# Windowed attention joined to a Mish MLP on one core: the first two pairs' scores, exponentials and squares stand beside the first layer, and the second layer has four attention visits in place of five

## The chip, the cores and the metric

The kernel runs on one core of a Trainium2 chip. The metric is the device time of one execution in microseconds (us). Before the change it is 1049.76 us, the median of three runs. The engines are named as in the profile: PE (TensorE's matmuls) and PEld (its weight loads), DVE (VectorE), ACT (ScalarE), POOL (GpSimd) and SP (SyncE, whose queue issues all the DMAs here).

## The reference

```python
B, H, S, D = 8, 8, 576, 64
scores = scale * np.matmul(q, k.transpose(0, 1, 3, 2))
bias = slopes[:, None, None] * (-np.abs(rel))[None, :, :]
mask = (rel >= 0) & (rel < 128)
scores = np.where(mask, scores + bias[None], -1000000000.0)
attn = np.exp(scores - np.max(scores, axis=-1, keepdims=True))
attn = attn / (np.sum(attn, axis=-1, keepdims=True) + 1e-09)
x = (attn @ v).transpose(0, 2, 1, 3).reshape(B * S, H * D)      # 4608 x 512
h = x @ w_in                                                    # 512 x 2048
sp = np.where(h > 20.0, h, np.log1p(np.exp(np.minimum(h, 20.0))))
out = (h * np.tanh(sp)) @ w_out                                 # 2048 x 512
```

Attention looks back over 127 positions at most, so each block of 128 queries meets 192 keys at a time. The MLP's weights come as 64-bit numbers.

## The kernel before

**Two halves of the work.** The attention of one batch gives 576 rows of x. 512 of them go through the MLP as one unit `c`; the last 64 queries of every batch are kept in DRAM (`xs`) and make a ninth unit, `c` = 8. A unit has a **first layer**, eight chunks `j` of 24 matmuls 128x512 into `h` (`first(c, j)`), each followed by a Mish on ACT (`mish`, g<-h); and a **second layer**, 32 steps of 6 matmuls into `po0` and `po1` (`second`), 16 for each half of the rows. What the second layer multiplies is prepared by `parts`: a rounded copy on ACT and a remainder on POOL (both gg<-g), three buffers. A finished `po0` or `po1` is copied to `ob` and stored; each has one bank.

**Attention of the next batch stands inside the unit.** `attention(b)` makes the steps of the four pairs of heads `p` of batch `b` = `c` + 1, for `c` = 1 to 6. A pair goes through these steps, in two groups `g` of blocks:

- `scores`: 36 matmuls 64x64 with `qk`. Pair 0 writes the banks `o`, `w`, `po0`, `po1`; the others write `s`, whose two buffers the first layer's `h` uses too.
- `bias`: twelve DVE instructions, pz<-s,nb, into the tile `pz` (tag `pz`, two buffers, one for each group).
- `exp`: nine ACT instructions in place, each with a sum. `divide` and `scale`: the sums plus 1e-9 (ACT), their reciprocal (DVE), the product (POOL).
- `turn` and `move_out`: DVE transposes squares of 32 in place, and three DMAs write `pz` to DRAM (`d`). `move_in`: six DMAs read `d` back as the transposed weights, into `pta` and `ptb`, which have one buffer each.
- `rest_values` and `values`: 60 small matmuls of `pta` and `ptb` with `v` into `o` and `w`. `keep` copies the last 64 queries to `xo` and stores them in `xs`; `split_x` makes the MLP's input x from `o` and `w` (ACT and DVE).

**Where they stand.** PE and SP work through the program in its written order; on DVE, ACT and POOL the framework's scheduler orders the instructions when the kernel is built. Pair 0's scores and biases are written ahead of the first layer's last chunk. Everything else is sorted into the 32 steps of the second layer by a number:

```python
VISITS = (2.0, 10.0, 16.5, 23.0, 29.9)
def when(x):
    k = min(max(int(x // 1), 0), 3)
    return VISITS[k] + (VISITS[k + 1] - VISITS[k]) * (x - k)
```

So pair 1's scores come at step 2.0, the values of pair 0 and the scores of pair 2 at 10.0, the values of pair 1 and the scores of pair 3 at 16.5, and the values of pairs 2 and 3 at 23.0 and 29.9. A pair's `move_in` and the loads of a later pair's `qk` are written shortly behind such a visit, and `keep` ahead of them. `v` of pairs 0 and 1 is loaded at the start of the second layer, into the tiles from which the first layer read x.

**The start.** Batches 0 and 1 and the MLP of unit 0 follow an order written out by hand (`FIRST_STEPS`), on all engines; the weights are converted to two rounded parts there (cE, cW, cU, cL: ACT and DVE, ACT, POOL, with tiles `ti`, `wi`, `si`; `to`, `wo`, `so` for the second layer's). In it, `lC0` to `lC3` copy the last queries of batch 0's pairs to `xo` (three buffers), and `lbS0` to `lbS3` are batch 1's scores of the last queries: matmuls of a block of `qk`, 128 columns called the corner, that stands behind q and k in each `qk` tile of 640 KB. The `xs` stores stand in SP's queue behind the loads of all weights but one.

Of the kernel before, what the change touches and what calls it, by code (L numbers as in the profile page):

```python
# [8 lines left out]
F32 = mybir.dt.float32  # L9
# [7 lines left out]
P = 128  # L17
# [63 lines left out]
def attention_mish_mlp(  # L81
# [23 lines left out]
    B, NP, _, QKZ = qk_.shape  # L105
    NT, DM = out.shape
    S = NT // B
# [7 lines left out]
    LEFT = S - CH  # L115
# [49 lines left out]
    def load(dst, src):  # L165
        sp.dma_start(out=dst, in_=src)
# [90 lines left out]
    qkv = {}  # L257
# [10 lines left out]
    def parts_of(t):  # L268

        qk = t[:, : 2 * S].rearrange("p (a s) -> p a s", a=2)  # L270
        return lambda h, n0, n: qk[h, 0, n0 : n0 + n], lambda h, n0, n: qk[h, 1, n0 : n0 + n], t[:, 2 * S : QKZ]

    def tables_of(t, l):
        return t.bitcast(BF16).rearrange("p (i n) -> p i n", i=2), l.bitcast(BF16)

    def load_first(p):

        t = tiles[p]
        if p > 1:
            n = QKZ + TAB + LAST  # L280
            load(t[:, :n], qk23[p - 2])
            qkv[(0, p)] = (*parts_of(t), *tables_of(t[:, QKZ : QKZ + TAB], t[:, QKZ + TAB : n]))
            return


        pieces = []
        n = 0
        for k in (CH, TAB, 6 * P, P, LAST):
            pieces.append(t[:, n : n + k])
            n += k  # L290
        a, tab, b, z, l = pieces
        load(a, qka[p])
        load(tab, tabs[p])
        if p == 0:
            load(b, qkb0)
        else:
            load(last_of(tiles[0]), last0)
            load(t[:, CH + TAB : n], qkb1)
        q = lambda h, n0, n: a[h, n0 : n0 + n] if n0 < 256 else b[h, n0 - 256 : n0 - 256 + n]
        k = lambda h, n0, n: a[h, 256 + n0 : 256 + n0 + n] if n0 + n <= 256 else b[h, 192 + n0 : 192 + n0 + n]  # L300
        qkv[(0, p)] = (q, k, z, *tables_of(tab, l))
# [3 lines left out]
        return t[:, n : n + P + LAST]  # L305

    def load_pair(b, p):
        t = at.tile([P, QKZ], F32, tag="qk", name=f"qk{b}_{p}")
        load(t, qk_[b, p])
        qkv[(b, p)] = parts_of(t)  # L310

    def load_v(b, p):

        pl, tag = (at, "pta") if (b, p) == (0, NP - 1) else (xp, f"x{p}")
        t = pl.tile([P, 2, 4, P], F32, tag=tag, name=f"v{b}_{p}", bufs=1)
        load(t, v[b, p])
        qkv[("v", b, p)] = ((t[:, 0], t[:, 1]), t[:64, 1, 3])

    def score_banks(name):
        return ps.tile([P, 2, 512], F32, tag="s", name=f"s{name}", bufs=2)  # L320
# [159 lines left out]
    def last_unit(p):  # L480
# [3 lines left out]
        name = f"{b}_{p}l"  # L484

        def scores():
            _, keys, z = qkv[(b, p)]

            t = qkv[("s", b, p)] = score_banks(f"{b}_{p}_0")
            st["s"] = t[:, :, :96]  # L490
            for a in range(2):
                for r in HEAD:
                    pe.matmul(
                        st["s"][r, a, :], lhsT=z[:, r], rhs=keys(slice(0, P), 384 + 96 * a, 96),
                        start=True, stop=True, skip_group_check=True,
                    )
# [54 lines left out]

        def keep():
            o = st["o"]
            xo = at.tile([P, LEFT], F32, tag="xo", name=f"xo{name}", bufs=3)
            dve.tensor_copy(xo, o)
            sp.dma_start(out=xs[p, :, b * LEFT : (b + 1) * LEFT], in_=xo)

# [10 lines left out]
    def pair_steps(b, p):  # L568
# [9 lines left out]
            return 256 * a if g == 0 else (384, 192)[a]  # L578

        def scores(g):  # L580
            if p == 0:

                tags = ("po0", "po1") if g else "ow"
                s_ = [ps.tile([P, 512], F32, tag=x, name=f"{x}s{name}") for x in tags]
            else:
                t = score_banks(f"{name}_{g}")
                s_ = [t[:, i, :] for i in range(2)]
            st[g]["s"] = s_
            q, k, _ = qkv[(b, p)]
            for a, j in enumerate(GROUPS[g]):  # L590
                for u in range(2):
                    q0 = j * P + 64 * u
                    k0, n = (q0 - WINDOW, SPAN) if j else (0, P)
                    for i in range(2):
                        pe.matmul(
                            s_[i][HALF[u], group_col(g, a) : group_col(g, a) + n],
                            lhsT=q(HEAD[i], q0, 64), rhs=k(HEAD[i], k0, n),
                            start=True, stop=True, skip_group_check=True,
                        )
            if g:  # L600
                for i in range(2):
# [136 lines left out]
                )  # L738

        def keep():  # L740
            xo = at.tile([P, LEFT], F32, tag="xo", name=f"xo{name}", bufs=3)
            dve.tensor_copy(xo, qkv[("o", b, p)][1][:, 2 * P : 2 * P + LEFT])
            sp.dma_start(out=xs[p, :, b * LEFT : (b + 1) * LEFT], in_=xo)

# [11 lines left out]
        exps = [[(lambda g=g, a=a, i=i: block_exp(g, a, i)) for a in ((1, 0) if g else (0, 1)) for i in range(2)] for g in range(2)]  # L756
        biases[1].insert(2, last_bias)
        exps[1].insert(2, last_exp)
        begin = [lambda: scores(0), lambda: scores(1)]
        if p == 0:  # L760
            begin += biases[0] + biases[1]
            both = [(0.8 + 0.05 * g, f) for g in range(2) for f in exps[g]]
        else:
            both = [(0, begin[0]), (0.001, begin[1])]
            both += [(0.01 + 0.05 * g, f) for g in range(2) for x in zip(biases[g], exps[g]) for f in x]
        d = 0.7 if p == 0 else 0
        both += [
            (d + 0.12, lambda: divide(0)), (d + 0.125, lambda: scale(0)),
            (d + 0.2, lambda: divide(1)), (d + 0.21, lambda: scale(1)),
            (d + 0.3, lambda: turn(0)), (d + 0.31, lambda: move_out(0)),  # L770
            (d + 0.45, lambda: turn(1)), (d + 0.46, lambda: move_out(1)),
            (d + 0.6 if p == 0 else 1.01, lambda: move_in(0)), (d + 0.7 if p == 0 else 1.02, lambda: move_in(1)),
            (2.002, rest_values), (2.003, values), (2.01, keep), (2.02, split_x),
        ]
        return begin, both

    def first_attention():

# [102 lines left out]
        def last_queries(p):  # L881
# [56 lines left out]
                        )  # L938

            def keep():  # L940
                xo = at.tile([P, LEFT], F32, tag="xo", name=f"xo{name}", bufs=3)
                dve.tensor_copy(xo, st["o"])
                sp.dma_start(out=xs[p, :, :LEFT], in_=xo)

# [13 lines left out]

    def attention(b):

        VISITS = (2.0, 10.0, 16.5, 23.0, 29.9)

        def when(x):
            k = min(max(int(x // 1), 0), 3)
            return VISITS[k] + (VISITS[k + 1] - VISITS[k]) * (x - k)

        steps = []
        for p in range(NP):
            begin, rest = pair_steps(b, p)
            if p == 0:  # L970
                first_scores = begin
            steps += [(when(p - 1 + d), f) for d, f in rest]
            nxt = (b, p + 2) if p + 2 < NP else (b + 1, p + 2 - NP)
            if nxt[0] < B:
                steps.append((when(p - 0.97), lambda nxt=nxt: load_pair(*nxt)))

        steps += [(d, lambda p=p: load_v(b, p)) for p, d in enumerate((-0.5, -0.4, 4.0, 17.5))]
        return first_scores, sorted(steps, key=lambda s: s[0])

    def last_x():  # L980
        c = B
# [161 lines left out]
    for name in FIRST_STEPS.split():  # L1143
        steps[name]()
        if name in loads:
            loads[name]()
        if name == f"Q{NJ - 1}":
            load_w(*last_w)
            add_conversions(range(len(conv) - 2, len(conv)))
            for p in range(2):  # L1150
                load_v(1, p)
    dve.fixed = act.fixed = pool.fixed = False

    for c in range(1, B + 1):
        for j in range(NJ):
            if j == NJ - 1:
                parts(c, 0, 0)
                parts(c, 0, 1)
                if c + 1 < B:
                    first_scores, beside = attention(c + 1)  # L1160
                    for f in first_scores:
                        f()
            if c > 1 or j > 2:
                first(c, j)
            if c > 1 or j > 1:
                mish(c, j)

        n = 4 * NJ
        steps = []
# [3 lines left out]
            if m >= 2:  # L1173
                steps.append((2 * m - 4.1, lambda m=m: parts(c, *divmod(m, NJ))))
        if c + 1 < B:
            steps += beside
        elif c + 1 == B:
            steps.append((4.5, last_x))
        for _, work in sorted(steps, key=lambda s: s[0]):
# [89 lines left out]
```

## Time and profile before

| | us |
|---|---|
| Three runs | 1045.5, 1049.76, 1049.86 |
| Profiled execution: its own time | 1039.15 |
| Its span, first to last instruction | 1037.4 |
| PE busy in the span | 952.7 |
| First layer of unit 3, with pair 0's scores | 45.26 |
| Second layer of unit 3, with attention | 72.64 |
| Second layer of unit 7, without attention | 43.52 |

The profiled execution is 1.75 us longer than its span, and 10.6 us shorter than the runs' median. PE is busy for 92% of the span, and what it waits for is read layer by layer: the first layers and the second layers are different stages, and so is the start.

### The profile page before, as it was taken

To read this page: it belongs to the slowest core of one execution; us is meant where nothing else is said; L and a number is where in the kernel's file an instruction comes from. 1 tells how busy PE (TensorE), PEld (TensorE's weight loads), DVE (VectorE), ACT (ScalarE), POOL (GpSimd) and SP (SyncE) were. 2 spreads that over 40 slices of the span, in tenths; PEclk is the share of its full clock that TensorE was granted. 3 is DMA by queue.
4 is the path that set the end of the run, shared out by engine and by line. 5 is a ranking of instruction groups with operands and counts; after the bars stand their busy time and mean duration, and the time that the engine had idled before them with its cause. 6 is when DMAs were issued, how large, how long until landed. Compare 5 with 4: busy or idle time off the path is not lost.

```text
span 1037.4 us, 17207 instructions
## 1 busy us (share of the span) xinstructions
PE 952.7 (92%) x6650; PEld 778.0 (75%) x6650; DVE 286.9 (28%) x1119; ACT 403.3 (39%) x1051; POOL 330.1 (32%) x300
## 2 busy tenths in 40 slices
PE   9859999979899799979899799979899799999998
PEld 7648788867788677867788577867788688888886
DVE  6568861135101530134101530134101530100000
ACT  7668752155123532155123432155123433221221
POOL 5438751044211541044211540044211541042032
PEclk9969999998999899989999899998999899999999
DMA  9941320045501661054501661055501651000001
GB/s 350 398 166 49 110 91 23 26 156 154 148 1 67 178 203 38 28 168 136 152 1 67 177 203 37 26 162 144 154 0 67 198 146 43 21 21 21 1 1 40
DMA packets 89217, 108.20 MB, mean 104 GB/s; under 512 B 22704, under 2 KB 69296, under 8 KB 89136
## 3 DMA queue, kind: packets, MB, share of 16 engines
q1 hardware_dynamic: 89136, 107.11, 32.6%
q8 instruction: 52, 0.85, 0.3%
q14 instruction: 29, 0.24, 0.1%
HBM read 76.94 MB, written 30.15 MB: 103 GB/s over the span
## 4 chain that ended last, share of the span: by engine, by line
PE 52%; issue 16%; DMA 14%; SPq 6%; DVE 5%; ACT 3%; POOL 3%; DVEq 0%; POOLq 0%; ACTq 0%
PE h L69 25%; PE po L69 21%; DMA d<-pz 7%; SPq L69 6%; DVE pz L69 4%; DMA pta<-d 3%; DMA wi<-in_moe_w_in_dram 2%; PE o L69 2%; PE w L69 2%; POOL pz L69 2%; PE s L69 2%; DMA nb<-in_relb_dram 1%; POOL gg L69 1%; ACT pz L69 1%; ACT g L69 1%
## 5 line engine op out<-in xcount | busy, mean ns | idle before, releaser
L69 PE MATMUL po<-so,gg 128*128 128x512 f32 x1728 | 411.5, 396 | 6.8 <-POOL gg L69 6.0
L69 PE MATMUL h<-x,si 128*128 128x512 f32 x1728 | 398.7, 392 | 17.3 <-ACT g L69 17.3
L69 PEld LDWEIGHTS h<-x,si 128*128 128x128 f32 x1728 | 325.1, 189 | 86.8 <-ACT g L69 17.7
L69 PEld LDWEIGHTS po<-so,gg 128*128 128x128 f32 x1728 | 324.0, 190 | 80.4 <-POOL gg L69 8.1
L69 POOL TENSOR_TENSOR gg<-g,gg 128x512 fp32r<-128x512 f32 x144 | 184.2, 1286 | 552.3 <-ACT gg L69 534.6
L69 ACT ACTIVATE g<-h 128x1024 f32<-128x1024 f32 x72 | 74.0, 1027 | 266.6 <-PE h L69 266.6
L69 ACT ACTIVATE pz<-pz,mx 128x192 f32<-128x192 f32 (+1 forms) x280 | 120.4, 431 | 89.1 <-DVE mx L69 86.2
L69 ACT ACTIVATE gg<-g 128x512 fp32r<-128x512 f32 x144 | 89.4, 627 | 126.4 <-PE po L69 124.3
L69 POOL TENSOR_TENSOR pz<-pz,sm 128x256 f32<-128x256 f32 (+4 forms) x96 | 96.9, 1030 | 96.6 <-DVE sm L69 87.9
L69 DVE CUSTOM_DVE_ANT_0 pz<-s,nb 128x192 f32<-128x192 f32 (+1 forms) x220 | 65.4, 328 | 71.1 <-DMA d<-pz 62.0
L69 DVE CUSTOM_DVE_ANT_0 pz<-os,nb 128x192 f32<-128x192 f32 x12 | 4.3, 355 | 226.6 <-PE ws L69 226.6
L69 DVE STREAM_TRANSPOSE pz<-pz 128x768 f32<-128x768 f32 (+2 forms) x72 | 49.9, 719 | 40.8 <-POOL pz L69 40.6
L69 PE MATMUL s<-qk 64*64 64x192 f32 (+2 forms) x808 | 44.0, 330 | 16.2 <-DVE mx L69 15.2
L69 ACT ACTIVATION_READ_ACCUMULATOR pz<-pz,mx 128x1 f32 x280 | 52.5, 187 | 0.0
L69 PEld LDWEIGHTS s<-qk 64*64 64x64 f32 (+1 forms) x808 | 31.7, 139 | 26.8 <-issue 22.1
L69 PE MATMUL w<-pta,v 64*64 64x64 f32 x288 | 17.4, 249 | 36.8 <-DMA pta<-d 36.8
L69 DVE COPY ob<-po 128x512 f32<-128x512 f32 x10 | 6.9, 691 | 137.0 <-PE po L69 137.0
L69 PE MATMUL o<-pta,v 64*64 64x64 f32 (+1 forms) x768 | 43.4, 250 | 0.2 <-DMA ptb<-d 0.2
L69 PEld LDWEIGHTS w<-pta,v 64*64 64x64 f32 x288 | 14.0, 154 | 39.0 <-DMA pta<-d 25.4
L69 PEld LDWEIGHTS o<-pta,v 64*64 64x64 f32 (+1 forms) x768 | 36.4, 156 | 7.1 <-issue 3.5
L69 ACT ACTIVATE x<-o 128x256 fp32r<-128x256 f32 (+1 forms) x32 | 13.0, 405 | 64.9 <-PE w L69 64.4
L69 ACT ACTIVATE ob<-po 128x512 f32<-128x512 f32 x26 | 15.6, 599 | 43.1 <-PE po L69 43.1
(186 smaller groups left out, 533.6 us busy)
## 6 DMA issues: line engine op xcount, KB each, us to landing
qk<-in_qk_dram SPq DMA_DIRECT2D x28, 640.0 KB, 5.0
v<-in_v_dram SPq DMA_DIRECT2D x32, 512.0 KB, 5.4
d<-pz SPq DMA_DIRECT2D x24, 384.0 KB, 3.3
pta<-d SPq DMA_DIRECT2D x72, 128.0 KB, 2.8
wi<-in_moe_w_in_dram SPq DMA_DIRECT2D x16, 512.0 KB, 10.9
wo<-in_moe_w_out_dram SPq DMA_DIRECT2D x16, 512.0 KB, 10.2
out_dram<-ob SPq DMA_DIRECT2D x32, 256.0 KB, 2.3
d<-pz SPq DMA_DIRECT2D x24, 320.0 KB, 4.8
```

Of the source, the lines that this page charges most:

```text
L69: ins = method(*args, **kwargs)
```

## The change

- Pairs 0 and 1 move their first half into the first layer. Ahead of chunk 4 (pair 0) and chunk 6 (pair 1) stand their scores, now both in `o`, `w`, `po0`, `po1`, and their biases; between the chunk's matmuls and its Mish their exponentials, `divide` and `scale`; behind the Mish `turn` and `move_out`. Pair 0's `move_in` stands behind chunk 5's Mish. The loads of the `qk` that take their buffers stand ahead of chunks 4 and 6.
- The second layer has four visits, at 5.0, 13.3, 21.6 and 29.9: the values of one pair each, and the scores of pairs 2 and 3 at the first two. Behind a visit SP's queue has `move_in`, then the `qk` load, then the `xs` store.
- `qk` is loaded without its corner. Batch 1, which alone uses corners, loads those of its four pairs in one DMA (`load_corners`), issued behind two loads of `v` once unit 0's first layer has been written; its tile is `pta`.
- `xo` has five buffers in place of three.
- `v` of pair 2 is loaded at step 6.5 in place of 4.0.

```diff
@@ -305,8 +305,8 @@
     def load_pair(b, p):
-        t = at.tile([P, QKZ], F32, tag="qk", name=f"qk{b}_{p}")
-        load(t, qk_[b, p])
+        t = at.tile([P, 2 * S], F32, tag="qk", name=f"qk{b}_{p}")
+        load(t, qk_[b, p][:, : 2 * S])
         qkv[(b, p)] = parts_of(t)
...
+    corners = {}
+
+    def load_corners(b):
+
+        t = corners[b] = at.tile([P, 2, 4, P], F32, tag="pta", name=f"z{b}", bufs=1)
+        load(t[:, 0], qk_[b, :, :, 2 * S :].rearrange("a p n -> p a n"))
...
-            xo = at.tile([P, LEFT], F32, tag="xo", name=f"xo{name}", bufs=3)
+            xo = at.tile([P, LEFT], F32, tag="xo", name=f"xo{name}", bufs=5)
...
         def scores(g):
-            if p == 0:
+            if p < 2:
...
+        ends = [(0, rest_values), (0.001, values), (0.008, keep), (0.009, split_x)]
+        ends = [(p + d, f) for d, f in ends]
+        if p < 2:
+            before = [both_scores] + biases[0] + biases[1]
+            beside = exps[0] + [lambda: weights(0)] + exps[1] + [lambda: weights(1)]
+            behind = [lambda: squares_out(0), lambda: squares_out(1)]
+            return before, beside, behind, in_out, ends
+        steps = [(-0.001, both_scores)]
+        steps += [(0.01 + 0.05 * g, f) for g in range(2) for x in zip(biases[g], exps[g]) for f in x]
+        steps += [(0.12 + 0.09 * g, lambda g=g: weights(g)) for g in range(2)]
+        steps += [(0.3 + 0.15 * g, lambda g=g: squares_out(g)) for g in range(2)]
+        steps += [(1.005, in_out)]
+        return [(p - 2 + d, f) for d, f in steps] + ends
...
-        VISITS = (2.0, 10.0, 16.5, 23.0, 29.9)
+        VISITS = (5.0, 13.3, 21.6, 29.9)
...
+            before, beside, behind, in_out, ends = pair_steps(b, p)
+
+            ahead[4 + 2 * p] = (before + [lambda p=p: next_pair(p)], beside, behind)
+            if p:
+                steps.append((0.005, in_out))
+            else:
+                ahead[5] = ([], [], [in_out])
+            steps += ends
+        steps = [(when(x), f) for x, f in steps]
+
+        steps += [(d, lambda p=p: load_v(b, p)) for p, d in enumerate((-0.5, -0.4, 6.5, 17.5))]
...
+            for work in before:
+                work()
             if c > 1 or j > 2:
                 first(c, j)
+            for work in beside:
+                work()
             if c > 1 or j > 1:
                 mish(c, j)
+            for work in behind:
+                work()
```

**ACT in the first layer of unit 3.** The rows run from the Mish of chunk 3 on (g3_1<-h3_3); pz4_0 and pz4_1 are pairs 0 and 1 of batch 4, and a table load stands wherever ACT passes from Mish to exp or back. Before:

```order
L69 ACTIVATE g3_1_3759<-h3_3_3785 128x1024
L69 ACTIVATE g3_2_3812<-h3_4_3811 128x1024
L69 ACTIVATE g3_2_3812<-h3_5_3838 128x1024
L69 ACTIVATE g3_3_3865<-h3_6_3864 128x1024
L69 ACTIVATE g3_3_3865<-h3_7_3937 128x1024
L69 ACT_TABLE_LOAD
```

And now:

```order
L69 ACTIVATE g3_1_3765<-h3_3_3791 128x1024
L69 ACT_TABLE_LOAD
L69 ACTIVATE pz4_0_0_3829,sm4_0_0_3828<-pz4_0_0_3829,mx4_0_0_3827 128x6x32 x4
L69 ACTIVATE sm4_0_1_3843<-sm4_0_1_3843 128x5
L69 ACT_TABLE_LOAD
L69 ACTIVATE g3_2_3860<-h3_4_3859 128x1024
L69 ACTIVATE g3_2_3860<-h3_5_3911 128x1024
L69 ACT_TABLE_LOAD
L69 ACTIVATE pz4_1_0_3957,sm4_1_0_3956<-pz4_1_0_3957,mx4_1_0_3955 128x6x32 x4
L69 ACTIVATE sm4_1_1_3971<-sm4_1_1_3971 128x5
L69 ACT_TABLE_LOAD
L69 ACTIVATE g3_3_3988<-h3_6_3987 128x1024
```

Two sets of nine exponentials (of which the first four are shown, and the copy of the sums that ends each set) stand between the Mish instructions, with four more table loads in a layer.

**SP's queue at the visits of the second layer of unit 2** (batch 3's pairs). Before, from the store of pair 0's last queries on:

```order
L69 DMA xs_95<-xo3_0_3285 128x64
L69 DMA pta3_1_3288<-d03_1_3171 64x4x128 x3
L69 DMA ptb3_1_3289<-d13_1_3184 64x4x160 x2
L69 DMA pta3_1_3288<-d23_1_3185 64x4x96
L69 DMA qk4_0_3309<-in_qk_dram 128x1280
L69 DMA d03_2_3347<-pz3_2_0_3238 128x3x256
```

And now:

```order
L69 DMA pta3_1_3250<-d03_1_3101 64x4x128 x3
L69 DMA ptb3_1_3251<-d13_1_3105 64x4x160 x2
L69 DMA pta3_1_3250<-d23_1_3106 64x4x96
L69 DMA qk4_0_3258<-in_qk_dram 128x1152
L69 DMA xs_95<-xo3_0_3260 128x64
L69 DMA v3_2_3301<-in_v_dram 128x1024
L69 DMA d03_2_3314<-pz3_2_0_3197 128x3x256
```

The six reads and the `qk` load moved ahead of the `xs` store, and pair 2's `v` came behind it.

**SP's queue in the start**, at the loads of batch 1's `v` (v_0, v_1) behind unit 0's first layer; z is the tile of the corners:

```order
 L69 DMA v_0_1054<-in_v_dram 128x1024
 L69 DMA v_1_1056<-in_v_dram 128x1024
-L69 DMA qk_2_1133<-in_qk_dram 128x1280
-L69 DMA v_2_1336<-in_v_dram 128x1024
+L69 DMA z_1058<-in_qk_dram 128x4x128
+L69 DMA qk_2_1135<-in_qk_dram 128x1152
+L69 DMA v_2_1338<-in_v_dram 128x1024
```

The corners' load came into the queue behind both `v` loads; before, those of pairs 0 and 1 had come with `qk_0` and `qk_1`, seven and six DMAs earlier, and those of pairs 2 and 3 with their own `qk`.

## Rows read from the trace of the kernel before

**Rows 1.** Page, part 1: busy time, share of the span, instructions.

```profile
PE 952.7 (92%) x6650; PEld 778.0 (75%) x6650; DVE 286.9 (28%) x1119; ACT 403.3 (39%) x1051; POOL 330.1 (32%) x300
```

**Rows 2.** Windows, six second layers: us, busy PE/PEld/DVE/ACT/POOL, PEclk, DMA; sum.

```profile
441.50:514.14 72.64, 61.26 (x542) 49.44 (x541) 24.87 (x105) 30.46 (x105) 29.03 (x25) 0.93 0.52 154
...
sum 426.11, PE 367.08 PEld 297.72 DVE 149.54 ACT 183.23 POOL 174.56; mean PE 61.18 PEld 49.62 DVE 24.92 ACT 30.54 POOL 29.09
```

**Rows 3.** Windows: a first layer with pair 0's scores; a second layer without attention.

```profile
396.24:441.50 45.26, 45.26 (x229) 37.16 (x228) 3.59 (x24) 10.97 (x12) 3.83 (x3) 1.00 0.10 31
902.15:945.67 43.52, 43.52 (x193) 36.05 (x193) 2.11 (x4) 11.49 (x18) 16.76 (x13) 1.00 0.07 25
```

**Rows 4.** Waits of PE, second layer of unit 3: us in total, times, longest.

```profile
PE w L69 <- DMA pta<-d: 6.5, 3, 3.6
PE s L69 <- DVE mx L69: 2.4, 1, 2.4
PE po L69 <- POOL gg L69: 1.7, 1, 1.7
PE po L69 <- ACT gg L69: 0.9, 1, 0.9
```

**Rows 5.** Timeline of PE: around a visit without a wait; behind a wait.

```profile
833.86 9.84 PE L69 MATMUL po<-so,gg 128*128 128x512 f32 x42
...
845.43 8.45 PE L69 MATMUL po<-so,gg 128*128 128x512 f32 x36
...
470.65 8.85 PE L69 MATMUL po<-so,gg 128*128 128x512 f32 x36
```

**Rows 6.** Timelines of PE, DVE and SP at the visit of 16.5, unit 3.

```profile
482.74 7.12 PE L69 MATMUL po<-so,gg 128*128 128x512 f32 x30
485.00 0.36 DVE L69 CUSTOM_DVE_ANT_0 pz<-s,nb 128x192 f32<-128x192 f32 x1 [8.81 <-DMA d<-pz]
489.07 0.22 DVE L69 COPY xo<-w 128x64 f32<-128x64 f32 x1
489.75 1.91 SPq L69 DMA_DIRECT2D pta<-d  x3
```

**Rows 7.** ACT: Mish (page, part 5), table loads (groups); first and last of nine exponentials.

```profile
L69 ACT ACTIVATE g<-h 128x1024 f32<-128x1024 f32 x72 | 74.0, 1027 | 266.6 <-PE h L69 266.6
L69 ACT ACT_TABLE_LOAD x15 | 19.2, 1283 | 0.3
444.06 0.45 ACT L69 ACTIVATE pz<-pz,mx 128x192 f32<-128x192 f32 x1
447.53 0.39 ACT L69 ACTIVATE pz<-pz,mx 128x128 f32<-128x128 f32 x1
```

**Rows 8.** Biases (page, part 5); one pair's products (timeline); a write of `d` (DMA issues).

```profile
L69 DVE CUSTOM_DVE_ANT_0 pz<-s,nb 128x192 f32<-128x192 f32 (+1 forms) x220 | 65.4, 328 | 71.1 <-DMA d<-pz 62.0
449.86 3.17 POOL L69 TENSOR_TENSOR pz<-pz,sm 128x768 f32<-128x768 f32 x3
d<-pz SPq DMA_DIRECT2D x4, 320.0 KB, 6.1
```

**Rows 9.** Timelines of SP, DVE, ACT and PE in the start.

```profile
51.97 0.33 SPq L69 DMA_DIRECT2D xs<-xo_0l  x1
61.10 0.22 DVE L69 COPY xo_3l<-pt_3l 128x64 f32<-128x64 f32 x1 [19.09 <-DMA xs<-xo_0l]
61.41 0.62 ACT L69 ACTIVATE ti<-wi 128x512 f32<-128x512 f32 x1 [18.62 <-issue]
64.42 34.99 PE L69 MATMUL h<-x,si 128*128 128x512 f32 x144 [17.25 <-ACT g L69]
```

**Rows 10.** Batch 1's `v`: issue, landing (by tile); the last queries' first scores on PE.

```profile
99.86 0.90 SPq L69 DMA_DIRECT2D v<-in_v_dram  x2
DMA to landing us min/median/max: 6.0/6.4/6.8
102.06 1.91 PE L69 MATMUL s<-qk 128*64 128x96 f32 x40
```

More of the change, by code (lines that the diff above doesn't have):

```diff
@@ L270, in parts_of @@
         qk = t[:, : 2 * S].rearrange("p (a s) -> p a s", a=2)
-        return lambda h, n0, n: qk[h, 0, n0 : n0 + n], lambda h, n0, n: qk[h, 1, n0 : n0 + n], t[:, 2 * S : QKZ]
+        return lambda h, n0, n: qk[h, 0, n0 : n0 + n], lambda h, n0, n: qk[h, 1, n0 : n0 + n]
     def tables_of(t, l):
@@ L281, in load_first @@
             load(t[:, :n], qk23[p - 2])
-            qkv[(0, p)] = (*parts_of(t), *tables_of(t[:, QKZ : QKZ + TAB], t[:, QKZ + TAB : n]))
+            qkv[(0, p)] = (*parts_of(t), t[:, 2 * S : QKZ], *tables_of(t[:, QKZ : QKZ + TAB], t[:, QKZ + TAB : n]))
             return
@@ L486, in scores @@
         def scores():
-            _, keys, z = qkv[(b, p)]
+            keys, z = qkv[(b, p)][1], corners[b][:, 0, p]
             t = qkv[("s", b, p)] = score_banks(f"{b}_{p}_0")
@@ L588, in scores @@
             st[g]["s"] = s_
-            q, k, _ = qkv[(b, p)]
+            q, k = qkv[(b, p)]
             for a, j in enumerate(GROUPS[g]):
@@ L740, in keep @@
         def keep():
-            xo = at.tile([P, LEFT], F32, tag="xo", name=f"xo{name}", bufs=3)
+            xo = at.tile([P, LEFT], F32, tag="xo", name=f"xo{name}", bufs=5)
             dve.tensor_copy(xo, qkv[("o", b, p)][1][:, 2 * P : 2 * P + LEFT])
@@ L758, in pair_steps, with both_scores, weights, squares_out @@
         exps[1].insert(2, last_exp)
[L759 to L775, printed above, removed]
+        def both_scores():
+            scores(0)
+            scores(1)
+        def weights(g):
+            divide(g)
+            scale(g)
+        def squares_out(g):
+            turn(g)
+            move_out(g)
+        def in_out():
+            move_in(0)
+            move_in(1)
+        ends = [(0, rest_values), (0.001, values), (0.008, keep), (0.009, split_x)]
[11 more added lines that the diff above has]
+        return [(p - 2 + d, f) for d, f in steps] + ends
     def first_attention():
@@ L940, in keep @@
             def keep():
-                xo = at.tile([P, LEFT], F32, tag="xo", name=f"xo{name}", bufs=3)
+                xo = at.tile([P, LEFT], F32, tag="xo", name=f"xo{name}", bufs=5)
                 dve.tensor_copy(xo, st["o"])
@@ L959, in attention, with next_pair @@
     def attention(b):
-        VISITS = (2.0, 10.0, 16.5, 23.0, 29.9)
+        VISITS = (5.0, 13.3, 21.6, 29.9)
         def when(x):
-            k = min(max(int(x // 1), 0), 3)
+            k = min(max(int(x // 1), 0), 2)
             return VISITS[k] + (VISITS[k + 1] - VISITS[k]) * (x - k)
[L967 to L972, printed above, removed]
+        def next_pair(p):
             nxt = (b, p + 2) if p + 2 < NP else (b + 1, p + 2 - NP)
             if nxt[0] < B:
-                steps.append((when(p - 0.97), lambda nxt=nxt: load_pair(*nxt)))
-        steps += [(d, lambda p=p: load_v(b, p)) for p, d in enumerate((-0.5, -0.4, 4.0, 17.5))]
-        return first_scores, sorted(steps, key=lambda s: s[0])
+                load_pair(*nxt)
+        ahead, steps = {}, []
+        for p in range(NP):
+            if p > 1:
+                steps += pair_steps(b, p) + [(p - 1.993, lambda p=p: next_pair(p))]
+                continue
+            before, beside, behind, in_out, ends = pair_steps(b, p)
[7 more added lines that the diff above has]
+        steps += [(d, lambda p=p: load_v(b, p)) for p, d in enumerate((-0.5, -0.4, 6.5, 17.5))]
+        return ahead, sorted(steps, key=lambda s: s[0])
     def last_x():
@@ L1151, in attention_mish_mlp @@
                 load_v(1, p)
+            load_corners(1)
     dve.fixed = act.fixed = pool.fixed = False
     for c in range(1, B + 1):
+        ahead, steps_beside = attention(c + 1) if c + 1 < B else ({}, [])
         for j in range(NJ):
+            before, beside, behind = ahead.get(j, ([], [], []))
             if j == NJ - 1:
@@ L1158, in attention_mish_mlp @@
                 parts(c, 0, 1)
[L1159 to L1162, printed above, removed]
+            for work in before:
+                work()
             if c > 1 or j > 2:
                 first(c, j)
+            for work in beside:
+                work()
             if c > 1 or j > 1:
                 mish(c, j)
+            for work in behind:
+                work()
         n = 4 * NJ
@@ L1175, in attention_mish_mlp @@
         if c + 1 < B:
-            steps += beside
+            steps += steps_beside
         elif c + 1 == B:
```

## The prediction

> **What bounds the kernel now.** PE is busy for 952.7 of 1037.4 us [rows 1], so at most 85 us of waiting can go, and the question is which stage holds it. Cut into stages, the answer is plain: in a first layer PE is busy for all 45.26 us and its clock is granted in full (1.00); in the second layer behind it PE is busy for 61.26 of 72.64 us and the mean clock is 0.93 [rows 2, 3]. There are six such second layers, 426.11 us together [rows 2].
>
> What they would take without waits follows from undisturbed rows. A second layer alone is 43.52 us [rows 3]. One pair's scores are the difference between a first layer with them and a layer without: 45.26 - 43.52 = 1.74 us [rows 3]. One pair's values are what lies between the steps on both sides of a visit without a wait: 845.43 - (833.86 + 9.84) = 1.73 us [rows 5]. With three scores and four values that is 43.52 + 5.22 + 6.92 = 55.66 us, six times 334.0. So 92.1 us, 15.4 a layer, are waits and what follows from them.
>
> The list of PE's waits in one layer names them: 6.5 us in three waits for the transposed weights (`pta`), 2.4 for the biases that must free a bank, 2.6 for the parts of the second layer's input [rows 4]: 11.5 in all, as 72.64 - 61.26 says too. The busy time above the bare work, 61.26 - 55.66 = 5.6 us, goes with the clock: behind the longest wait 36 matmuls of the second layer still take 8.85 us against 8.45 undisturbed [rows 5], and the mean clock of the stage is 0.93.
>
> The third stage is the start. DVE waits 19.09 us for `xo`, because the store that frees it stands behind the weight loads and is issued only at 51.97; ACT's next conversion waits for the bank that this copy frees (18.62), the first Mish for ACT, and PE 17.25 us for the Mish [rows 9]. One small copy with too few buffers holds all engines.
>
> **The change, part by part.** *The scores of pair 1* move from a second layer to a first one: 1.74 us off one and onto the other, nothing in the sum. The first layer then has 43.52 + 3.48 = 47.0 us, the second 43.52 + 3.48 + 6.92 = 53.9.
>
> *The waits for `pta`.* They come from short distances and from the queue. At the visit of 16.5 the values end at 482.74, but the next pair's six reads are issued from 489.75 on: they stand behind the `xs` store, whose copy (489.07) stands on DVE behind pair 3's biases, which wait 8.81 us for an earlier write of `pz` to land [rows 6]. Now the reads stand ahead of the store and need only the values' end and the write that they read. Six issues at 0.64 us (1.91 / 3 [rows 6]) and a landing no longer than a write's 6.1 [rows 8] make 10; the next visit is 8.3 steps later, 8.3 x 1.36 (43.52 / 32) = 11.3 us, the first time with scores besides. The write is in time too: from the start of a pair's scores at one visit, half the scores (0.9), twelve biases of 0.33 with the exponentials beside them, products of 3.17, and a write of 6.1 us [rows 8] come to 14.1, some 17 with the transposes and issues between them; the reads are wanted two visits and 8 steps later, 2 x 3.47 + 10.9 = 17.8 us. Late next would be the reads, which have 11.3 - 10 = 1.3 us to spare, or more where they land sooner than a write. So these 6.5 us go. Pair 0's chain has four chunks of 5.44 us (43.52 / 8) and five steps, pair 1's two chunks and a visit more.
>
> *The wait for a bank* (2.4 us) goes with pair 1's scores: only two pairs use `s` in the second layer, 11 us apart.
>
> *The waits for parts* (2.6 us) need not all go. ACT and POOL have two pairs' work beside the second layer in place of four, but a new neighbour appears: the visit at 13.3 ends two steps before the half ends, so that ACT copies out `po0` behind nine exponentials of pair 3. The last bias ends 0.9 + 12 x 0.33 = 4.8 us after the scores' start, and two exponentials, pair 1's two x copies and the eviction follow on ACT; PE wants the bank at 1.74 + 1.73 + 2 x 1.36 = 6.2. That is short by about an instruction or two; the nearest row is the 0.9 us for which PE waits today for an ACT behind exponentials [rows 4]. It is more if pair 2's write, which frees `pz`, lands late. I keep 1.2 us a layer for all that is left, between 0 and 5 (today's 2.4 + 2.6). The clock's loss goes with the long waits.
>
> *On ACT in the first layer* the exponentials and four more table loads stand ahead of the Mish. They are hidden, and the cover is the second `h` bank. Counted from a chunk's scores: Mish of the chunk before (1.03), table (1.28), nine exponentials that take 447.53 + 0.39 - 444.06 = 3.9, table again [rows 7]: 7.5, about 8 us with the two copies of the sums. The chunk's own matmuls end at 7.2, so Mish is done at 9, and its bank is wanted again at 12.6 or later. The cover is gone, and each us costs one, once ACT is over 3.6 us later.
>
> *`xo`.* With five buffers the copy need not wait. DVE goes on 19.09 us earlier, PE 17.25 us, and its next 144 matmuls take 144 x 0.227 (43.52 / 192) = 32.6 in place of 34.99 [rows 9]: 19.6 on PE. What could be late in its place is the weights: the store issued at 51.97, behind them in the queue, has landed by 61.10 [rows 9], so the last of them are in near 60, and they were issued in the order in which the conversions want them. I take 19, between 15 and 20.
>
> *Corners.* Their load is a new wait. The two `v` loads are issued from 99.86 to 100.76 and land after 6.0 and 6.8 us, at 107.1 [rows 10]; the corners come behind them in the same queue, while PE wants them at 102.06 [rows 10], both 19 us earlier now. From below the wait is nothing, if they land 1.3 us after their issue; from above they take half of `v`'s longer time once more (they are half its size), and land at 110.5: 8.4 us. They share the queue with `v`, so its landing is the nearest row; I take that and one more us, 6, and 1 us for the clock behind such a gap: 7, between 0 and 9. PE, DVE and ACT all follow the hand-written order behind it, so that nothing else moves up.
>
> *The smaller `qk` loads, pair 2's `v` and the table loads at the start* cost nothing: DMA is busy for 0.52 of a second layer [rows 2], and of loads PE waits for none now [rows 4].
>
> **Sum.** 92.1 - 6 x 1.2 = 84.9 from the layers, 19 from the start, less 7 for the corners: 96.9. Against the profiled execution's own 1039.15 us that is 942.3; against the runs' median, 10.6 us above it, 952.9. The rows cannot tell whether those 10.6 us go with the waits, so I take the middle, **948 us**.
>
> **A rule that speaks against the change.** ACT's fifteen table loads take 1.283 us each, with 0.3 us of idle time ahead of all of them together [rows 7]. The Trainium skill, "ScalarE: Activation LUTs", *Rules for kernel authors*, says to group functions by table set and to finish one set before switching; the change does the opposite 24 times. The Trainium skill, same title, *What ACT_TABLE_LOAD costs*, adds a drain of 1.38 us to each; by that, as an estimate, ACT is 2.8 us later at each Mish in question, which is inside the 3.6 us of cover; the row shows no such drain.
>
> **The rivals.**
>
> - *Waits that move* (the evictions and parts of the second layer): all of today's other 5.0 us a layer stay, 948 + 6 x 3.8 = 971 us. For it: ACT's order, with the evictions behind nine exponentials and x copies; against it: ACT and POOL are busy for 30 and 29 of 73 us [rows 2], with twice the pairs.
> - *The table loads come onto the path*: 24 x 1.28 = 31, so 979 us. For it: they stand between Mish instructions, on which `h`'s banks depend; against it: 3.6 us of cover each. This is where the rule of the Trainium skill named above would show.
> - *The start gains nothing*: the change does not do there what it says, because what the conversions read, or the stores, are late too. 948 + 19 = 967 us. For it: the store issued at 51.97 needs 9 us behind the loads [rows 9], so DMA is full until 61; against it: the weights that are wanted next were issued first.
> - *Slower*: pair 1's biases wait for pair 0's write, since `pz` has two buffers; ACT stands with nine exponentials ahead of chunk 6's Mish, and pair 2's scores stand on PE until that bank is free. The bank is wanted 1.74 + 10.9 + 6.8 = 19.4 us after pair 1's scores begin, and ACT needs some 8 of them, so PE waits once the write lands over 11 us after those scores begin, and the kernel is slower than before from 11 + 101 / 6 = 28 us on. Against it: writes land in about 6 us [rows 8] and are issued before those scores.
>
> **How the numbers follow.** The sum as it stands has 62 in 100, waits that move 17, the start 9, table loads 7, slower 1, and 4 for less than the sum (no waits left, corners in time: 932). The likeliest case alone reaches from 936 (all waits gone, and the 10.6 us with them) to 962. The range takes in the start and most of the waits that move: 935 to 972. About 0.5% is what a measurement of this kernel can tell from no change, 5 us; every case but the last is far beyond it: faster 0.97, same 0.015, slower 0.015.
>
> **What would show it.** Right: no wait of PE for `pta` over 0.5 us in the second layers, each 54 to 57 us with a clock near 1.00; first layers of 47.0 without a wait; PE without its gap of 17 us near 47; one new gap of some 6 us ahead of the last queries' first scores, near 83. Wrong: PE waiting for Mish (h <- g) in chunks 6 or 7 or at pair 2's scores; gaps ahead of `po` at step 16, with ACT's evictions late; a second layer over 60 us.

## The result, and the profile after

The changed kernel takes 952.84 us, the median of four runs (951.43 to 953.14), against 1047.63 (1043.97 to 1049.86) of the kernel before on the same chip: a ratio of 0.910, 95% interval 0.906 to 0.913. Its profiled execution took 953.0 us, in a span of 951.2.

The page of the changed kernel, part 1, answers to [rows 1]:

```profile
PE 931.4 (98%) x6650; PEld 759.8 (80%) x6650; DVE 284.6 (30%) x1119; ACT 434.5 (46%) x1075; POOL 332.0 (35%) x300
```

PE does the same 6650 matmuls in 21.3 us less busy time, and waits 20 us where it waited 85. The stages say where (windows; a first layer, then two second layers of the six and their sum; answers to [rows 2, 3]):

```profile
357.71:405.07 47.36, 47.36 (x266) 38.58 (x265) 11.81 (x58) 24.61 (x56) 10.26 (x9) 1.00 0.30 91
...
301.25:357.71 56.46, 55.36 (x506) 45.03 (x505) 16.45 (x71) 22.05 (x65) 22.98 (x19) 1.00 0.49 143
405.07:461.85 56.78, 55.38 (x506) 45.02 (x505) 16.51 (x71) 22.41 (x65) 22.99 (x19) 1.00 0.47 141
...
sum 337.26, PE 332.16 PEld 270.14 DVE 98.56 ACT 132.70 POOL 137.94; mean PE 55.36 PEld 45.02 DVE 16.43 ACT 22.12 POOL 22.99
```

The second layers fell from 426.11 to 337.26 us, at full clock; the first layers took on pair 1's scores and still wait for nothing. PE's waits over the whole span (total, times, longest), where [rows 4] had four kinds in one layer:

```profile
PE s L69 <- DMA z<-in_qk_dram: 6.0, 1, 6.0
PE po L69 <- ACT ob L69: 5.1, 6, 1.4
```

No wait for `pta` is left, and every other wait of PE is 1.1 us at most. The first row is the corners (z), the second the eviction behind pair 3's exponentials, once in each of six layers. In the start, PE's 17.25 us gap [rows 9] is gone, and the corners' gap stands where the prediction put it (timelines of SP and PE):

```profile
80.61 0.90 SPq L69 DMA_DIRECT2D v<-in_v_dram  x2
81.55 0.45 SPq L69 DMA_DIRECT2D z<-in_qk_dram  x1
...
80.00 2.88 PE L69 MATMUL po<-so,gg 128*128 128x512 f32 x12
88.90 0.91 PE L69 MATMUL s<-qk,z 128*64 128x96 f32 x8 [6.02 <-DMA z<-in_qk_dram]
```

On ACT the table loads went from 15 to 39 [rows 7], and Mish instructions are not late: in the page's part 5 the first layer's matmuls, which waited 17.3 us for ACT before, wait 0.0.

```profile
L69 PE MATMUL h<-x,si 128*128 128x512 f32 x1728 | 398.2, 390 | 0.0
L69 ACT ACT_TABLE_LOAD x39 | 50.0, 1283 | 13.9 <-DVE mx L69 13.4
```

### The profile page after: what moved, and what is told of

Same layout as the page of the kernel before. It is cut to its first block, busy times and chain, and to the rows that moved or that the text cites. A ratio compares the mean times of both kernels' runs of the same rounds, so it can differ in the third digit from the quotient of the medians.

```text
span 951.2 us, 17253 instructions
## 1 busy us (share of the span) xinstructions
PE 931.4 (98%) x6650; PEld 759.8 (80%) x6650; DVE 284.6 (30%) x1119; ACT 434.5 (46%) x1075; POOL 332.0 (35%) x300
## 4 chain that ended last, share of the span: by engine, by line
PE 89%; ACT 5%; DMA 3%; DVE 1%; issue 1%; POOL 1%; SPq 0%; DVEq 0%; ACTq 0%; POOLq 0%
PE h L69 40%; PE po L69 38%; PE s L69 3%; PE o L69 3%; ACT pz L69 3%; DMA d<-pz 1%; PE w L69 1%; PE po0s L69 1%; PE os L69 1%; DMA v<-in_v_dram 1%; DMA z<-in_qk_dram 1%; DVE pz L69 1%; SPq L69 0%; ACT x L69 0%; POOL pz L69 0%
## 5 line engine op out<-in xcount | busy, mean ns | idle before, releaser
L69 PEld LDWEIGHTS h<-x,si 128*128 128x128 f32 x1728 | 323.0, 188 | 70.3 <-issue 3.3
L69 DVE CUSTOM_DVE_ANT_0 pz<-s,nb 128x192 f32<-128x192 f32 (+1 forms) x160 | 46.9, 328 | 107.6 <-PE s L69 84.5
L69 ACT ACT_TABLE_LOAD x39 | 50.0, 1283 | 13.9 <-DVE mx L69 13.4
L69 DVE CUSTOM_DVE_ANT_0 pz<-os,nb 128x192 f32<-128x192 f32 x24 | 8.5, 355 | 151.5 <-PE ws L69 151.5
L69 DVE COPY xo<-w 128x64 f32<-128x64 f32 x24 | 5.4, 224 | 116.1 <-PE w L69 115.7
L69 PEld LDWEIGHTS o<-pta,v 64*64 64x64 f32 (+1 forms) x768 | 27.7, 136 | 8.1 <-issue 6.4
L69 PE MATMUL o<-pta,v 64*64 64x64 f32 (+1 forms) x768 | 32.8, 226 | 0.0
L69 DVE DVE_READ_ACCUMULATOR2_ANT mx<- 128x1 f32 (+1 forms) x360 | 29.0, 81 | 0.0
L69 PE MATMUL s<-qk 64*64 64x192 f32 (+1 forms) x560 | 28.0, 326 | 0.0
```

Of the source, the lines that this page charges most:

```text
L69: ins = method(*args, **kwargs)
```

## The experiments

The theory is the prediction's sum: the start gains 19 us and gives 7 back at the corners; in the layers, spacing, queue order and the two moved pairs together take PE's waits away, and the table loads are hidden. The rivals: one of these parts carries the gain and the others nothing, and the start or the table loads come out otherwise.

**The start.** e1 gives the kernel before five `xo` buffers and `load_corners` with smaller `qk` tiles, and nothing else; e7 gives the changed kernel three buffers again:

```diff
-            xo = at.tile([P, LEFT], F32, tag="xo", name=f"xo{name}", bufs=5)
+            xo = at.tile([P, LEFT], F32, tag="xo", name=f"xo{name}", bufs=3)
```

> The kernel before with the change's start alone: five xo buffers, qk without its corner, the corners' load behind the two v loads; layers, visits and queue order as before. If one small copy with three buffers held the start, as the prediction says, it gains 19 us and gives 6 to 7 back at the corners: 12 to 13 us faster than the kernel before, some 1035 against 1047.6, with PE's 17 us gap near 47 gone and a gap of 6 us near 83. The rival, that the start gains nothing because what the conversions read is late too, gives no change or 6 us more, 1047 to 1054.

Measured: 1029.34 us against 1046.43, ratio 0.983 (0.977 to 0.989); in the profiled execution the span is 12.4 us shorter than that of before. PE goes through the first layer without its gap, and waits 6.5 us for the corners:

```profile
41.12 38.40 PE L69 MATMUL h<-x,si 128*128 128x512 f32 x168
...
88.77 0.91 PE L69 MATMUL s<-qk,z 128*64 128x96 f32 x8 [6.53 <-DMA z<-in_qk_dram]
```

> The changed kernel with xo back at three buffers. If the buffers are what the start gained, the 17 us gap of PE near 47 returns and with it 17 to 20 us: 970 to 973 in place of 953. If the start's gain came from something else in the change (the smaller qk loads, the corners), it stays at 953.

Measured: 970.7, ratio 0.928 (0.923 to 0.932), and one wait of that old kind (PE's waits):

```profile
PE h L69 <- ACT g L69: 17.7, 1, 17.7
```

So the buffers alone are worth 17.9 us (970.7 - 952.84), and the start as a whole 12 us by the profiled executions and 17 by the medians (1046.43 - 1029.34). That the start gains nothing is refuted from both sides.

**Order, spacing and pairs.** Four runs undo or do the parts of the layers one by one: e3 writes `keep` ahead of the reads (0.008 becomes 0.004), e4 sets the four visits back to their old places, e10 does both, and e11 puts the kernel before's `keep`, and `split_x` with it, behind its reads (2.01 becomes 2.035).

```diff
-        ends = [(0, rest_values), (0.001, values), (0.008, keep), (0.009, split_x)]
+        ends = [(0, rest_values), (0.001, values), (0.004, keep), (0.009, split_x)]
...
-        VISITS = (5.0, 13.3, 21.6, 29.9)
+        VISITS = (10.0, 16.5, 23.0, 29.9)
```

> The changed kernel with the xs store back ahead of the six reads and the qk load at each visit; spacing and pairs as changed. By the prediction's chain (reads of 10 us, 11.3 between visits) the store's copy, which DVE makes some 3 us after the values behind the biases, makes the reads 3.5 us later and PE waits 2.2 us for pta at two visits of six layers: 26 us, 979. By the rows of the changed kernel the last read is issued 3.3 us after the first and lands 3.0 later, 6.4 in all, so that 3.5 more are still hidden by the 13.9 between visits: no change, 953.

Measured: 988.96, ratio 0.947 (0.941 to 0.952). Order matters by 36 us (31 between the profiled executions), but neither expectation had the mechanism: no wait for `pta` comes back, PE waits 28.7 us for `ob`. In unit 3 (timelines of DVE, SP and PE):

```profile
433.52 0.23 DVE L69 COPY xo<-w 128x64 f32<-128x64 f32 x1
446.95 0.36 DVE L69 CUSTOM_DVE_ANT_0 pz<-s,nb 128x192 f32<-128x192 f32 x1 [11.08 <-DMA d<-pz]
...
433.77 0.33 SPq L69 DMA_DIRECT2D xs<-xo  x1
434.20 1.91 SPq L69 DMA_DIRECT2D pta<-d  x3
...
440.02 1.91 SPq L69 DMA_DIRECT2D d<-pz  x3
...
452.55 2.93 PE L69 MATMUL po<-so,gg 128*128 128x512 f32 x6 [5.11 <-ACT ob L69]
```

The store waits for a copy that stands on DVE behind pair 2's biases. Behind the store stand reads and loads, and behind those pair 2's writes of `d`, issued only at 440.02. They free `pz`, so pair 3's biases start at 446.95, their exponentials follow on ACT, and the eviction stands behind these. In the changed kernel the same rows are:

```profile
420.39 0.23 DVE L69 COPY xo<-w 128x64 f32<-128x64 f32 x1
429.21 0.36 DVE L69 CUSTOM_DVE_ANT_0 pz<-s,nb 128x192 f32<-128x192 f32 x1 [6.49 <-DMA d<-pz]
...
416.41 1.91 SPq L69 DMA_DIRECT2D pta<-d  x3
...
422.00 1.89 SPq L69 DMA_DIRECT2D d<-pz  x3
...
435.72 8.48 PE L69 MATMUL po<-so,gg 128*128 128x512 f32 x36 [1.40 <-ACT ob L69]
```

Here the reads are issued at 416.41, 4 us ahead of the copy, and the writes at 422.00, as soon as the transposes allow: these end at 422.72 here, and at 435.86 in e3, where the writes still stood in the queue for 4 us.

> The changed kernel with its four visits at the old places 10, 16.5, 23 and 29.9; pairs and queue order as changed. By the prediction's chain (reads of 10 us against 6.5 steps, 8.8 us) PE waits for pta some 1.1 us at two visits and 0.6 at one in six layers, 17 us, less the 5 us of waits for ob, which no longer stand behind a visit: 965. By the rows of the changed kernel (6.4 us from the first read's issue to the last landing) no wait for pta comes back and the waits for ob go: 948.

Measured: 947.64, ratio 0.905 (0.902 to 0.909), 5.2 us less than the changed kernel. No wait for `pta` or `ob`; a second layer is all work:

```profile
301.95:357.01 55.06, 55.06 (x506) 45.10 (x504) 16.39 (x71) 22.31 (x65) 23.02 (x19) 1.00 0.48 146
```

The wider spacing buys nothing and costs the eviction wait: the visit at 16.5 begins after the half's evictions, the one at 13.3 just before them.

> The changed kernel with both the old places of the four visits (10, 16.5, 23, 29.9) and the xs store ahead of the reads: of the change in the layers only the first halves of pairs 0 and 1 are left. By the mechanism that the run with the store first showed (pair 2's write of d stands behind the reads, and pair 3's biases wait for it to land), pair 3's exponentials end some 27 us after pair 2's scores, while the next visit wants the banks o and w that its x copies free at 24.6: a wait of about 3 us and one or two more for reads in six layers, some 970 to 978. If moving the two pairs is what took the waits away, and the order matters only where an eviction stands behind a visit, 948 to 953.

Measured: 984.8, ratio 0.941 (0.937 to 0.944), more than either expectation. The waits are spread over reads and the second layer's input (PE's waits):

```profile
PE w L69 <- DMA pta<-d: 9.7, 10, 1.8
PE po L69 <- POOL gg L69: 7.9, 5, 1.6
...
PE po L69 <- ACT gg L69: 5.0, 4, 1.8
```

> The kernel before with one edit: at each visit of the second layer the xs store stands behind the reads and the qk load, all else as before. If the order in the queue is most of the gain, as the 36 us of the run with the store first suggest, the reads of the visit at 16.5 start some 6 us earlier (489.75 against the values' end at 482.74 in the profile of before), the 39 us of waits for pta mostly go, and the time is near 1010. If the reads wait in any case for writes that biases hold up, since four groups of three pairs use pz in one second layer, nothing changes: 1042 to 1050.

Measured: 1016.11, ratio 0.970 (0.968 to 0.972): 31 us for one number (23 between the profiled executions). But the waits for `pta` did not mostly go, against the expectation: 26.4 us in six waits are left of 36.8 in sixteen. In the layer of unit 3 those that follow the reads of 16.5 are gone; what stays is the first visit's, and the bank (PE's waits, that layer; compare [rows 4]):

```profile
PE w L69 <- DMA pta<-d: 4.5, 1, 4.5
PE s L69 <- DVE mx L69: 2.4, 1, 2.4
```

The first visit's wait is the queue again. Three of pair 0's six reads are written behind pair 1's first write of `d`, and this waits for pair 1's transpose (timelines of DVE, SP and PE in e11, then SP and PE in the kernel before):

```profile
454.08 0.98 DVE L69 STREAM_TRANSPOSE pz<-pz 128x768 f32<-128x768 f32 x1
455.13 0.38 SPq L69 DMA_DIRECT2D d<-pz  x1
455.62 1.25 SPq L69 DMA_DIRECT2D ptb<-d  x2
456.92 0.61 SPq L69 DMA_DIRECT2D pta<-d  x1
459.84 0.37 PE L69 MATMUL w<-pta,v 64*64 64x64 f32 x1 [4.48 <-DMA pta<-d]
...
462.70 0.38 SPq L69 DMA_DIRECT2D d<-pz  x1
463.18 1.25 SPq L69 DMA_DIRECT2D ptb<-d  x2
467.49 0.36 PE L69 MATMUL w<-pta,v 64*64 64x64 f32 x1 [3.58 <-DMA pta<-d]
```

Pair 0's own writes have landed by 451.48 in e11, where pair 1's second group of biases goes on in the buffer that they free, so that some 4 of the 4.5 us are the queue's. In the kernel before, these first visits hold 24.3 of the 36.8 us. The change puts all six reads of pair 0 ahead of pair 1's write, and gives them more time as well; no run separates the two.

Ordered by what they contain, the medians make a ladder: before 1047; with the start 1029 (e1); with the two pairs moved and the fifth visit gone as well 985 (e10); with the order in the queue as well 947.6 (e4); with the wide spacing as well 952.8 (the change). The moved pairs are worth some 44 us, the order 37, the spacing minus 5; the shares depend on what is there already, since without the moved pairs the order is worth 31 (e11). By PE's rows the step from e1 to e10 takes away 26 us of waits for `pta`, 13 for the bank and 12 of busy time, and brings 6 of waits for the second layer's input.

**The table loads.** e5 adds four per chunk ahead of the Mish of chunks 4 and 6:

```diff
             for work in beside:
                 work()
+            for _ in range(2 if beside else 0):
+                act.activation(idle[:, 1:], idle[:, :1], AF.Mish)
+                act.activation(idle[:, 1:], idle[:, :1], AF.Exp)
```

> The changed kernel with four more table loads ahead of the Mish of chunks 4 and 6 (two small Mish and two small exponentials of a zero, whose results nothing reads): ACT gets there 4 x 1.283 and some 0.8 us later, 5.9 in all. With the prediction's cover of 3.6 us, both chunks cost 2.3 us in six layers: 28 us, 981. By the rows of the changed kernel Mish of chunk 4 is done 5.5 us before its bank is wanted and that of chunk 6 10 us: 2 to 3 us, 955. With a drain of 1.38 us for each load, as the Trainium skill has it (ScalarE: Activation LUTs, What ACT_TABLE_LOAD costs), ACT is 11.4 us later, and the estimate is 6 us for each chunk 4 and 1 for each chunk 6: 995.

Measured: 954.01, ratio 0.911 (0.908 to 0.913): 48 more loads cost 1.2 us by the medians. PE's waits show the edge of the cover, 0.5 us in each of six layers (the waits for `ob` give back 1.7 of these 3.0):

```profile
PE h L69 <- ACT g L69: 3.0, 6, 0.5
```

The timeline of ACT shows the added loads one behind the other:

```profile
284.43 0.20 ACT L69 ACTIVATE idle<-idle 128x1 f32<-128x1 f32 x1
284.75 1.28 ACT L69 ACT_TABLE_LOAD   x1
286.05 0.20 ACT L69 ACTIVATE idle<-idle 128x1 f32<-128x1 f32 x1
286.27 1.28 ACT L69 ACT_TABLE_LOAD   x1
```

Two instructions are 1.52 us apart from start to start (284.75 to 286.27), load, small activation and all. The cover is 5.9 - 0.5 = 5.4 us for chunk 4, and at least 5.9 for chunk 6. The drain of 1.38 us per load that the Trainium skill adds ("ScalarE: Activation LUTs", *What ACT_TABLE_LOAD costs*) doesn't show here; with it the estimate was 995.

**The price of a block.** e8 cuts each visit's values in two:

```diff
-        ends = [(0, rest_values), (0.001, values), (0.008, keep), (0.009, split_x)]
+        ends = [(-1.0 / 8.3, rest_values), (0.001, values), (0.008, keep), (0.009, split_x)]
```

> The changed kernel with each visit's values cut in two: the 24 small matmuls of the rest one step of the second layer ahead of the other 36, the same work in one block more per visit. If the price of a block that the prediction's 1.73 us left out (0.22 us on the 512-wide matmuls behind it) is one of passing from small matmuls to large ones, PE's busy time in a second layer rises by 4 x 0.22 = 0.9 us from 55.36 to 56.2, and the time by 5 us: 958. If it belongs to the small matmuls themselves, however they stand, PE stays at 55.36 and the time at 953.

Measured: 956.37, ratio 0.913 (0.911 to 0.915). The second layers (windows) hold the same matmuls in more busy time:

```profile
sum 339.87, PE 336.59 PEld 267.87 DVE 98.16 ACT 130.98 POOL 137.69; mean PE 56.10 PEld 44.65 DVE 16.36 ACT 21.83 POOL 22.95
```

That is 56.10 - 55.36 = 0.74 us a layer, 0.19 for each of four cuts: here a cut between small and 512-wide matmuls has a price.

**A version that beats both.** e2 moves the corners' load alone; e9 has the old visits besides; e12 joins scores and values as well.

```diff
                 load_v(1, p)
-            load_corners(1)
...
+    loads["lC3"] = lambda: load_corners(1)
...
-        steps = [(-0.001, both_scores)]
+        steps = [(0.002, both_scores)]
```

(The last pair of lines is e12's.)

> The changed kernel with one edit: the corners' load is written behind the store of pair 3's last queries of batch 0, some 20 us ahead of the two v loads instead of behind them. If the 6.0 us of PE's wait near 83 are the corners' landing alone, they go and nothing else takes their place: 946 to 947. If the v loads, the evictions or the Mish are as late, part of the gap stays under another name: 949 to 953.

Measured: 944.91, ratio 0.903 (0.901 to 0.905): 7.9 us, more than the 6.0 of the wait. The clock behind the gap explains it. Windows over the last queries' scores and the 48 matmuls of the second layer behind them, in the changed kernel:

```profile
88.90:92.30 3.40, 3.40 (x41) 2.34 (x41) 0.64 (x4) 0.47 (x3) 0.00 (x0) 0.50 0.03 5
92.30:104.05 11.75, 11.75 (x54) 9.70 (x51) 10.62 (x34) 9.98 (x31) 6.95 (x7) 0.94 0.16 50
```

And in e2, where they follow on without a gap:

```profile
81.86:83.70 1.84, 1.84 (x42) 1.41 (x41) 1.46 (x5) 1.33 (x3) 1.84 (x2) 1.00 1.00 301
83.70:94.88 11.18, 11.18 (x54) 9.23 (x51) 9.82 (x34) 11.05 (x34) 8.84 (x10) 1.00 0.33 128
```

After 6 us of idling PE works at a granted clock of 0.50, the level of 1.2 GHz, and takes 15.15 us for what takes 13.02 at 2.4 GHz: 2.1 us on top of the wait.

> The changed kernel with the visits at the old places (10, 16.5, 23, 29.9) and the corners' load ahead of the v loads, all else as changed. If the two edits are independent, the gains add: 947.6 less 6 to 7, some 941. If the earlier start of batch 1 runs into something that the corners hid, it stays between 942 and 948.

Measured: 940.6, ratio 0.899 (0.897 to 0.901): the gains add.

> The kernel of the run before in this call with the scores of pairs 2 and 3 directly behind the values at the same visit, in place of one step of six matmuls ahead of them: twelve blocks of small matmuls fewer in the whole program, the same work. If each block costs PE some 0.2 us at its border, as the run with the values in two suggests (4.6 us of busy time for 24 blocks), PE's busy time falls by 2.3 us and the time with it. If the border is free where the two blocks stand a step apart, or if the biases that begin 1.8 us later push pair 3's exponentials into an eviction, the time stays or rises by 1 to 3 us.

Measured: 939.35, ratio 0.897 (0.895 to 0.899), not told apart from e9. The edit took away six blocks, not the twelve of the expectation: at 16.5 scores and values already stood side by side. It also turned their order there, values first, so that two things changed. And the layer gained nothing: an undisturbed second layer takes 55.06 us in both (three of e9's six, all of e12's); e9 has two layers of 56.24 and 55.86 with waits for a part of its input (1.4 us together) that e12 doesn't have. The starts of PE's rows in one layer (e9's begins at 293.97, e12's at 293.74) say why:

```profile
309.34 1.65 PE L69 MATMUL po<-so,gg 128*128 128x512 f32 x6
312.73 8.46 PE L69 MATMUL po<-so,gg 128*128 128x512 f32 x36
324.42 9.84 PE L69 MATMUL po<-so,gg 128*128 128x512 f32 x42
...
312.27 8.50 PE L69 MATMUL po<-so,gg 128*128 128x512 f32 x36
324.18 9.86 PE L69 MATMUL po<-so,gg 128*128 128x512 f32 x42
```

Less 0.2267 us for each 128x512 matmul, scores and values at step 10 cost 312.73 - 293.97 - 14.96 = 3.80 us apart (e9) and 312.27 - 293.74 - 14.96 = 3.57 joined (e12). At 16.5, joined in both, they cost 3.53 with the scores first and 3.75 with the values first. So the join gained 0.23 and the turned order gave it back. No run has the join alone, and what sets the price stays open.

## Why the prediction held, and where its terms were off

The forecast was 948 with a range of 935 to 972; the median is 952.8. Its mechanism held in the main, but on the profiled execution's own time the sum gave 942.3 and 953.0 came: 10.7 us short, and the middle that it took hid half of that. That the forecast came within 5 us is therefore partly luck. The 10.6 us between the profile and the runs before did go: the changed kernel's profiled execution and its median agree to 0.2 us. But they did not go with the waits: in e11 PE still idles for 68 us (1014.4 - 946.2), and there too the two agree, to 0.4 us (1016.49 and 1016.11). What e11 shares with the change is the order in the queue.

Two rows of the kernel before bear on the second point below (timeline of PE; where a first layer begins, and the second layer behind it):

```profile
396.08 38.24 PE L69 MATMUL h<-x,si 128*128 128x512 f32 x168
...
441.52 4.24 PE L69 MATMUL po<-so,gg 128*128 128x512 f32 x18
```

- *The start*: 19 less 7. By the profile PE leaves unit 0's first layer 19.25 us earlier (80.0 against 99.25 before), the corners cost 6.0 and 2.1 for the clock, and a wait of 0.9 us for `mx_1l` goes: 12.05 net. Right, with its reasons; e7 and e2 measure 17.9 and 7.9.
- *The layers*: 84.9 was mis-sized by 11, mostly in the step "what they would take without waits". It put a second layer of two scores and four values at 53.9 us; e9 and e12 show 55.06 undisturbed, and 0.30 more once a wait breaks the row of matmuls (55.36). That is 1.46 in each of six layers, 8.8 us. The prices of 1.74 and 1.73 were read from the end of one block to the start of the next, while 128x512 matmuls overlap in the profile (390 ns each, one every 227). From start to start the kernel before's own first layer takes 441.52 - 396.08 = 45.44, so that a pair's scores are 1.92, and a first layer with two is 43.52 + 3.84 = 47.36, as measured, not 47.0: 1.8 in five. One pair's values, read so from [rows 5], are 845.43 - 833.86 - 42 x 0.2267 = 2.05. By these prices the second layer is 55.56, half a us above the 55.06 measured; most of that is the join at 16.5 (3.53 against 3.97). Another 2.5 us were never there: the second of the six windows of before began at 323.0, while its layer's first matmul starts at 325.5, so that 426.11 was too much. On the other side the waits left are 0.85 us a layer (5.1 / 6), not 1.2, which is 2.1. Together 8.8 + 1.8 + 2.5 - 2.1 = 11.0, within 0.3 of what came.
- *The waits for `pta`*: that they go was right, the weights of the reasons were not. The prediction leaned on distance, 11.3 us against reads of 10. The reads are issued within 4 us and land in 3 (medians of 2.8 to 3.2 in the page), and the old distance of 6.5 steps is enough (e4). What counts is that nothing late stands ahead in SP's queue (37 us). The prediction read the visit of 16.5 and found the store there; two thirds of the waits stood at the visit of 10, behind pair 1's write. The moved pairs take these away, and the bank's wait with them (44 us in all).
- *The order's second task* was named only as a risk ("more if pair 2's write, which frees `pz`, lands late"). It decides: with the store first, this chain makes PE wait 28.7 us for `ob` in place of 5.1, and costs 36 us by the medians (e3).
- *Waits for parts*: the eviction behind pair 3's exponentials came where the prediction put it; e4 shows that it belongs to the new place 13.3 and to nothing else.
- *Table loads*: hidden, as said, behind a cover of 5.4 us, not 3.6 (e5). The rule to group functions by table set (the Trainium skill, "ScalarE: Activation LUTs", *Rules for kernel authors*) speaks against the change; here ACT had room, and no wait of PE comes from the 24 loads.
- *Slower* by late biases in the first layer: no wait of `h` shows at all.

## What to carry to other kernels

In a queue that works in order, look first for an instruction that waits for a busy engine, and put behind it only what can wait as long: here one 32 KB store ahead of six reads cost more than the distances between the visits could give, and three reads behind another pair's write made two thirds of the waits for `pta`. Look at the largest wait of a kind, not at the first that fits. Before spreading work out in time, ask which shared buffer's release sets the chain. And read the price of a small block from start to start of the rows around it: their ends overlap, which hid about 1 us a layer here (six blocks, 390 less 227 ns each). A gap on PE costs its length and then the clock: 6.0 us became 7.9.

## What the runs showed of the hardware

- Behind a gap of 6.0 us the granted clock was 0.50 for 3.4 us and 0.94 over the next 11.75, against 1.00 without the gap.
- A table load and a 128x1 activation behind it took 1.52 us from one load to the next; all 87 loads of e5 have a mean of 1283 ns, as the 15 of before.
- A pair's scores as a block among 128x512 matmuls lengthened a first layer by 1.92 us (45.44 and 47.36 against 43.52). Four more cuts in a second layer added 0.74 us of busy time (55.36 to 56.10), and one short wait 0.30 (55.06 to 55.36). A pair's scores and another's values cost 3.80 us apart, 3.57 joined with the values first, and 3.53 at another visit with the scores first.
- The runs scatter by 5.9 to 10.9 us in the four kernels with the `xs` store ahead of the reads (before, e1, e3, e10), and by 0.6 to 4.7 in the nine with it behind, among them e11, in which PE waits for 68 us (1015.94 to 1016.49). Why stays open.
